# Attention into a two-layer feed-forward on one core: eight weight halves converted during the attention and kept in memory, six low parts moved to VectorE, and one step fewer in each conversion

## The chip, the cores and the metric

One core of a Trainium2 chip runs the whole program. The metric is the device time of one execution in microseconds (us). The kernel before takes 1147.3 us (median of three runs, 1147.26 to 1149.0). Differences up to 0.2%, about 2.3 us, are about what a measurement of this kernel cannot tell from no change.

The engines are named as in the profile: PE is TensorE's matrix product and PEld its weight load, DVE is VectorE, ACT is ScalarE, POOL is GpSimd, SP is the sync engine, whose queue issues nearly all transfers.

## The reference

A causal attention by blocks of 64, over 8 batches, 8 heads, 576 positions and head size 64; its output, as 4608 tokens of 512, goes through a feed-forward with 2048 hidden units and a leaky activation.

```python
scores = np.matmul(q, k.transpose(0, 1, 3, 2)) / np.sqrt(64)
scores = np.where(block_i >= block_j, scores, -1e9)
attn = np.exp(scores - scores.max(-1, keepdims=True))
attn = attn / (attn.sum(-1, keepdims=True) + 1e-09)
x = np.matmul(attn, v).transpose(0, 2, 1, 3).reshape(4608, 512)
h = x @ w_in
g = np.maximum(h, 0.0) + alpha * np.minimum(h, 0.0)
out = g @ w_out
```

The two weights reach the kernel as 64-bit floats, seen as pairs of 32-bit words. The kernel turns them into 32-bit floats itself.

## The kernel before, in words

**Products in two parts.** The kernel writes most operands of a product as a high part (a rounded copy, made on ACT) and a low part (the rest, a subtraction on POOL or DVE) and adds three products: high by high, low by high, high by low. `split` (L436) makes the two parts of a weight or of x: ACT at L438, POOL or DVE at L439.

**The hidden units in blocks.** The 2048 hidden units are 16 blocks f of 128. A block has two halves of weights, one of w_in and one of w_out, each 128 by 512. Blocks 0 to 5 (`first_weights`, L444) are converted at the start and stay in SBUF during the attention. The 32 pairs of heads (p = 0 to 31, four per batch) run through `query_tile` and `values`. Whenever the tokens of a batch are complete, chunks of 256 tokens (`chunk_a`, L634) go through blocks 0 to 5 between the steps of the attention (products at L518, L555) and their partial sums go to memory (`part`). x itself goes to memory too (`xd`).

**The second stage.** When the attention is over, its buffers are given back (`end_attention`, L1014), and blocks 6 to 15 are converted (`later_weights`, L460) while the last chunks of the first stage run; the w_in halves of blocks 6 and 7 alone have a low enough number (SOON) to be converted ahead, right behind the first six blocks. Then nine chunks of 512 tokens go through these ten blocks, two blocks at a time: `pair1` (L585) makes seven products in place of eight (L596) from sums and differences of quarters of the weights (L455) and of x (`factors`, L562), adds them on DVE (L605, L609), `activate` (L526) makes g (ACT L529, DVE L531), its high part gh (ACT L535) and its low part gl (POOL L538), and `ffn2` (L542) multiplies by w_out (L555). `store_out` (L1048) adds the partial sums.

**One conversion** (`to_f32`, L402) takes a half of 512 KB through six steps: DVE takes out the exponent (L416), ACT moves it (L419), DVE puts the sign on (L421), DVE takes out the mantissa as an integer into a PSUM bank (L425), ACT turns that integer into a float (L428), DVE adds the low word (L430) and multiplies by the power of two (L433). It holds two PSUM banks (eb, fb) from its first step to its last.

**What sets the order.** All this is a list of operations with priorities (the lower, the sooner). `Plan.schedule` runs through it with a cost for each operation, and for each engine, whenever that is free, takes the ready operation of lowest priority number for which buffers are free; buffers of the kinds in IN_ORDER are given in the order of the program. The result is one fixed order for each engine and for SP's queue. PSUM has eight banks, shared out by quotas: six for the attention (att), one each for the hidden units (hp) and the sums (acc); after the attention hp and acc have two each and the conversions four (words).

## Time and profile before

| | before |
|---|---|
| median of three runs | 1147.3 us |
| the profiled execution's own time | 1147.15 us |
| its span from first to last instruction | 1145.4 us |
| PE busy | 1119.7 us (98%) |
| PEld busy | 999.0 us (87%) |
| DVE busy | 844.1 us (74%) |
| ACT busy | 730.1 us (64%) |
| POOL busy | 612.1 us (53%) |
| transfers, mean | 127 GB/s |

Read it so: PE is idle for 25.7 us of the span, and where those lie decides what a change elsewhere can give. The stretches that matter are the start (0 to 120 us), the attention with the first six blocks (to about 596 us), the turn to the second stage (about 600 to 715 us, where blocks 6 to 15 are converted), and the second stage to the end.

### The profile page before, as it was taken

The numbers are of one execution on the slowest core, as the hardware profiler recorded it, in microseconds if no ns is written. First come the engines' busy times: TensorE is split into PE (matmuls) and PEld (weight loads), VectorE is DVE, ScalarE is ACT, GpSimd is POOL, SyncE is SP. The second block draws the span as 40 slices with busy tenths as digits, with TensorE's granted clock in tenths as the row PEclk, the third lists the DMA queues.
The fourth block names the chain that finished last, engine by engine and source line by source line (L and its number), as shares of the span: only waits on it lengthen the run. The fifth ranks groups of instructions, "written<-read, shape, count | busy, mean of one in ns | idle before, by whom it ended". The sixth has DMA issues, their size and how long they took to land. (4 is left out here: it accounts for less than half of the span.)

```text
span 1145.4 us, 22040 instructions
## 1 busy us (share of the span) xinstructions
PE 1119.7 (98%) x7288; PEld 999.0 (87%) x7288; DVE 844.1 (74%) x1968; ACT 730.1 (64%) x1950; POOL 612.1 (53%) x769
## 2 busy tenths in 40 slices
PE   7998999999999999999999989999999999999998
PEld 5666999999989999999998878988898889989887
DVE  8888899887887777778868999655657474656554
ACT  6887898987777887788865766443434343343432
POOL 5756556555565455556448987342425343342522
PEclk9999999999999999999999999999999999999999
DMA  8797676764745566557314442312122030302020
GB/s 229 218 258 234 172 215 175 205 176 113 228 133 151 163 180 183 132 142 226 88 48 165 144 143 74 116 37 74 41 71 78 34 111 1 111 16 95 2 74 37
DMA packets 74018, 145.86 MB, mean 127 GB/s; under 512 B 9648, under 2 KB 11440, under 8 KB 73904
## 3 DMA queue, kind: packets, MB, share of 16 engines
q1 hardware_dynamic: 73616, 144.31, 43.0%
q8 instruction: 58, 0.95, 0.4%
q14 instruction: 56, 0.46, 0.1%
q10 hardware_dynamic: 288, 0.14, 0.0%
HBM read 67.35 MB, written 28.31 MB: 84 GB/s over the span
## 5 line engine op out<-in xcount | busy, mean ns | idle before, releaser
L538 POOL TENSOR_TENSOR gl<-g,gh 128x256 fp32r<-128x256 f32 x288 | 223.2, 783 | 336.3 <-PE bank L596 159.6
L596 PEld LDWEIGHTS bank<-X,w 128*128 128x128 f32 x1890 | 253.6, 189 | 21.7 <-POOL X L439 1.1
L596 PE MATMUL bank<-X,w 128*128 128x256 f32 x1890 | 259.5, 281 | 1.3 <-POOL X L439 0.6
L555 PE MATMUL bank<-w,gh 128*128 128x512 f32 x720 | 225.8, 395 | 2.3 <-DVE g L531 1.3
L529 ACT ACTIVATE g<-bank 128x256 f32<-128x256 f32 x288 | 110.6, 385 | 158.2 <-DVE bank L609 142.0
L819 POOL TENSOR_SCALAR p<-p,ri 128x256 f32<-128x256 f32 (+3 forms) x256 | 146.0, 584 | 98.7 <-DVE ri L817 48.8
L535 ACT CAST gh<-g 128x256 fp32r<-128x256 f32 x288 | 116.9, 407 | 82.8 <-DVE g L531 81.6
L531 DVE SCALAR_TENSOR_TENSOR g<-g,oal,bank 128x256 f32<-128x256 f32 x288 | 136.0, 476 | 35.3 <-ACT g L529 29.4
L609 DVE TENSOR_TENSOR bank<-bank,g 128x256 f32<-128x256 f32 x180 | 76.0, 428 | 103.4 <-PE bank L596 102.4
L811 ACT ACTIVATE p<-bank,nm 128x256 f32<-128x256 f32 (+3 forms) x256 | 134.7, 531 | 27.0 <-DVE nm L808 11.8
L555 PE MATMUL bank<-w,gl 128*128 128x512 f32 x360 | 141.8, 394 | 1.4 <-POOL gl L538 1.4
L555 PE MATMUL bank<-wa,gh 128*128 128x512 f32 x432 | 140.9, 407 | 1.0 <-POOL wa L439 1.0
L555 PEld LDWEIGHTS bank<-w,gh 128*128 128x128 f32 x720 | 120.4, 188 | 15.4 <-DVE g L531 1.5
L518 PE MATMUL bank<-xh,wa 128*128 128x256 f32 x864 | 130.3, 288 | 0.0
L908 DVE TENSOR_TENSOR PL<-bank,PH 128x512 fp32r<-128x512 f32 (+2 forms) x189 | 111.1, 608 | 20.9 <-ACT PH L907 18.2
L518 PEld LDWEIGHTS bank<-xh,wa 128*128 128x128 f32 x864 | 114.1, 190 | 3.2 <-issue 0.4
L828 PE MATMUL bank<-ident,p 128*128 128x128 f32 x640 | 103.9, 280 | 6.6 <-POOL p L819 5.7
L795 PE MATMUL bank<-K,Q 128*128 128x512 f32 (+1 forms) x472 | 103.9, 335 | 0.0
L907 ACT CAST PH<-bank 128x512 fp32r<-128x512 f32 (+2 forms) x189 | 95.9, 529 | 11.8 <-PE bank L828 6.9
L828 PEld LDWEIGHTS bank<-ident,p 128*128 128x128 f32 x640 | 74.4, 142 | 19.7 <-POOL p L819 10.8
L605 DVE TENSOR_TENSOR g<-bank,g 128x256 f32<-128x256 f32 x135 | 56.6, 422 | 47.4 <-PE bank L596 46.5
L941 PE MATMUL bank<-PH,V 128*128 128x320 f32 x324 | 88.4, 288 | 0.0
(126 smaller groups left out, 2094.1 us busy)
## 6 DMA issues: line engine op xcount, KB each, us to landing
Q<-QH SPq DMA_DIRECT2D x62, 256.0 KB, 3.8
K<-KH SPq DMA_DIRECT2D x124, 128.0 KB, 3.6
vraw<-in_v SPq DMA_DIRECT2D x32, 320.0 KB, 3.1
qraw<-in_q SPq DMA_DIRECT2D x31, 320.0 KB, 3.6
xd<-xT SPq DMA_DIRECT2D x8, 1152.0 KB, 5.9
part<-o SPq DMA_DIRECT2D x36, 256.0 KB, 2.3
xb<-xd SPq DMA_DIRECT2D x9, 1024.0 KB, 5.3
m<-part SPq DMA_DIRECT2D x36, 256.0 KB, 3.3
```

The source lines that it names most:

```text
L518: nc.tensor.matmul(hp()[:, :n], ww()[:, 0, cc * P:(cc + 1) * P], x()[:, cc, :n], start=(i == 0 and cc == 0), stop=(i == 2 and cc == NCC - 1))
L529: op("ACT", c_act(CHA), lambda: nc.scalar.activation(out=g(), in_=hp()[:, ts], func=AF.Relu, scale=-1.0), r=[hp], w=[g], prio=FP)
L531: op("DVE", c_dve(CHA) + 60, lambda: nc.vector.scalar_tensor_tensor(out=g(), in0=g(), scalar=oal[:, f:f + 1], in1=hp()[:, ts], op0=ALU.mul ...
L535: op("ACT", c_act(CHA, True), lambda: nc.scalar.copy(out=gh(), in_=g()), r=[g], w=[gh], prio=FP)
L538: op("POOL", c_pool(CHA), lambda: nc.gpsimd.tensor_tensor(out=gl(), in0=g(), in1=gh().bitcast(F32), op=ALU.subtract), r=[g, gh], w=[gl], p ...
L555: nc.tensor.matmul(acc(), a()[:, ts], ww(), start=(first and i == 0), stop=(last and i == 2))
L596: nc.tensor.matmul(bank()[:, :CHA], W()[:, i, 256 * at + P * c:256 * at + P * c + P], B()[:, j, CHA * c:CHA * c + CHA], start=(n == 0), st ...
L795: nc.tensor.matmul(o, Q()[:, i, qs], K()[:, 2 * h + i, :w], start=(i == 0), stop=(i == 1))
L811: op("ACT", 238 + w / 1.2, lambda h=h, t=t: nc.scalar.activation(out=t()[:, :w], in_=sb[h]()[:, off[h]:off[h] + w], func=AF.Exp, bias=nm() ...
L819: op("POOL", 244 + w / 1.2, lambda h=h: nc.gpsimd.tensor_scalar(out=pts[h]()[:, :w], in0=pts[h]()[:, :w], scalar1=ri()[:, h:h + 1], scalar ...
L828: nc.tensor.transpose(out=tp()[:, base + c * P:base + (c + 1) * P], in_=pts[h]()[:, c * P:(c + 1) * P], identity=ident)
L908: op("DVE", c_dve(n) + (HALF if n == P else 0), lambda: nc.vector.tensor_tensor(out=lo(), in0=src(), in1=hi().bitcast(F32), op=ALU.subtrac ...
```

## The change

It has five parts.

1. In every conversion (32 halves) ACT's step L428 goes. DVE's next step reads the integer mantissa from PSUM and adds the low word times 2^-32; the last step, then a `scalar_tensor_tensor`, multiplies by 2^-20 and by the power of two.
2. Eight halves, those of w_in and w_out of blocks 8 to 11, are converted beside the attention, one each after pairs 12, 14, ... 26, with a priority number behind that of all nearby attention. Each result goes to a new tensor in memory (`wd`, 256 KB each), and `later_weights` loads it from there.
3. The low parts of the w_out halves of blocks 6 to 11 are subtracted on DVE and no longer on POOL.
4. After the attention hp has three banks and no longer two.
5. The plan is made anew with all this, so the order of every engine's work moves.

```diff
-BANKS, HB, AB, HT, AM, AT, WB = 6, 1, 1, 2, 2, 4, 4
+BANKS, HB, AB, HT, AM, AT, WB = 6, 1, 1, 3, 2, 4, 4
+AHEAD = {(8 + k // 2, k % 2): 12 + 2 * k for k in range(8)}
+    wd = dram.tile([2 * (NF - FA), P, 512], F32, name="wd")
...
-        op("ACT", c_act(512), lambda: nc.scalar.activation(out=fb(), in_=fb().bitcast(I32), func=AF.Copy, scale=2.0 ** -20),
-           w=[fb], prio=prio)
         op("DVE", c_dve(512), lambda: nc.vector.scalar_tensor_tensor(
-            out=mb(), in0=low(), scalar=2.0 ** -52, in1=fb(), op0=ALU.mult, op1=ALU.add),
+            out=mb(), in0=low(), scalar=2.0 ** -32, in1=fb().bitcast(I32), op0=ALU.mult, op1=ALU.add),
             r=[raw, fb], w=[mb], prio=prio)
-        op("DVE", c_dve(512), lambda: nc.vector.tensor_tensor(out=mb(), in0=mb(), in1=eb(), op=ALU.mult), r=[eb], w=[mb], prio=prio)
+        op("DVE", c_dve(512), lambda: nc.vector.scalar_tensor_tensor(
+            out=mb(), in0=mb(), scalar=2.0 ** -20, in1=eb(), op0=ALU.mult, op1=ALU.mult), r=[eb], w=[mb], prio=prio)
...
+    def weights_ahead(p):
+
+        for f, i in (k for k in AHEAD if AHEAD[k] == p):
+            pr = 5 * p + 100
+            mb, _ = to_f32((w_in, w_out)[i][f].bitcast(I32), pr, [("x", p // NP % 2, p % NP, 0, 1)])
+            at = 2 * (f - FA) + i
+            op("SP", 256, lambda mb=mb, at=at: nc.sync.dma_start(out=wd[at], in_=mb()), r=[mb], w=[("wd", f, i)], prio=pr)
+
+    def later(f, i, prio, after=(), use="att"):
+        if (f, i) not in AHEAD:
+            return to_f32((w_in, w_out)[i][f].bitcast(I32), prio, after, use)
+        mb, at = Buf("m"), 2 * (f - FA) + i
+        op("SP", 256, lambda: nc.sync.dma_start(out=mb(), in_=wd[at]), r=[("wd", f, i), *after], w=[mb], prio=prio)
+        return mb, mb
...
-                split(w, hi, lo, 512, [mb], (("w", f + i, 1), "h"), (("w", f + i, 1), "l"), [W], "POOL", prio(f) + .5)
+                split(w, hi, lo, 512, [mb], (("w", f + i, 1), "h"), (("w", f + i, 1), "l"), [W], "DVE" if f < 12 else "POOL", prio(f) + .5)
...
+        weights_ahead(p)
```

**The order, first place: DVE from the first sum of products in the second stage on.** `m` is a converted half, `raw` its words, `g` the hidden units, `X` a quarter of x. Before, in a row:

```order
L609 TENSOR_TENSOR bank_187<-bank_187,g_478 128x256
L439 TENSOR_TENSOR X_7981<-xt_7494,X_7981 128x512
L605 TENSOR_TENSOR g_687<-bank_221,g_478 128x256
L531 SCALAR_TENSOR_TENSOR g_610<-g_610,oal,bank_187 128x256
L416 TENSOR_SCALAR m_327<-raw_256 128x512
L425 TENSOR_SCALAR bank_247<-raw_256 128x512
L605 TENSOR_TENSOR g_7407<-bank_202,g_687 128x256
L605 TENSOR_TENSOR g_7429<-bank_240,g_687 128x256
L421 SCALAR_TENSOR_TENSOR bank_180<-raw_256,bank_180 128x512
L609 TENSOR_TENSOR bank_240<-bank_240,g_7407 128x256
L609 TENSOR_TENSOR bank_141<-bank_141,g_7429 128x256
L430 SCALAR_TENSOR_TENSOR m_327<-raw_256,bank_247 128x512
```

Now, from the same sum on (L609 is L625 there, L605 is L621, L531 is L547, L439 is L440):

```order
L625 TENSOR_TENSOR bank_188<-bank_188,g_7539 128x256
L621 TENSOR_TENSOR g_564<-bank_248,g_7539 128x256
L440 TENSOR_TENSOR X_8007<-xt_7567,X_8007 128x512
L547 SCALAR_TENSOR_TENSOR g_724<-g_724,oal,bank_188 128x256
L621 TENSOR_TENSOR g_505<-bank_142,g_564 128x256
L621 TENSOR_TENSOR g_7475<-bank_232,g_564 128x256
L625 TENSOR_TENSOR bank_232<-bank_232,g_505 128x256
L625 TENSOR_TENSOR bank_241<-bank_241,g_7475 128x256
L547 SCALAR_TENSOR_TENSOR g_7493<-g_7493,oal,bank_232 128x256
L625 TENSOR_TENSOR bank_203<-bank_203,g_505 128x256
L547 SCALAR_TENSOR_TENSOR g_7515<-g_7515,oal,bank_241 128x256
L547 SCALAR_TENSOR_TENSOR g_8083<-g_8083,oal,bank_203 128x256
```

Of the 24 rows from the first sum on, nine were steps of conversions; now two are. From the last row of the attention (L962) to the last step of the last conversion there were 173 rows of DVE with 18 conversions; now there are 137 with 10.

**Second place: DVE in the attention**, at the first of the eight halves. Before, the w_in halves of blocks 6 and 7 follow the first six blocks directly, and then no row of a conversion stands until the attention is over. Now these two come behind the eight, near the end of the attention, since `raw` and `m` are given in the order of the program. The first one's five DVE steps are spread over 24 rows, of which these are the last nine (L924 and L978 write parts of the attention's probabilities and outputs, L824 is a row maximum):

```order
L978 TENSOR_TENSOR xT<-bank_203,tmp_1312 64x320
L891 TENSOR_REDUCE sp_253<-s_138 128x1
L547 SCALAR_TENSOR_TENSOR g_564<-g_564,oal,bank_241 128x256
L893 RECIPROCAL ri_255<-sp_253 128x1
L430 SCALAR_TENSOR_TENSOR m_228<-raw_167,bank_248 128x512
L924 TENSOR_TENSOR PL<-bank_181,PH 128x2x128
L824 TENSOR_REDUCE nm_263<-bank_142 128x1
L824 TENSOR_REDUCE nm_263<-bank_188 128x1
L433 SCALAR_TENSOR_TENSOR m_228<-m_228,bank_232 128x512
```

The conversion takes the gaps that the attention leaves, and holds its two banks meanwhile; the longest of the eight spans 35 rows.

**Third place: SP's queue in the attention**, where it issues the loads of the next pair of heads. Before, in a row:

```order
L687 DMA K_128<-KL_323 64x512 x2
L672 DMA qraw_234<-in_q 128x640
L673 DMA kraw_245<-in_k 128x576
L659 DMA part<-o_164 128x512
L674 DMA vraw_170<-in_v 128x640
```

Now, at the second of the eight halves:

```order
L688 DMA qraw_235<-in_q 128x640
L689 DMA kraw_246<-in_k 128x576
L416 DMA raw_167<-in_w_in 128x1024
L675 DMA part<-o_154 128x512
L690 DMA vraw_171<-in_v 128x640
L703 DMA Q_126<-QH_293 64x2x512 x2
L703 DMA Q_126<-QL_320 64x512 x2
L688 DMA qraw_235<-in_q 128x640
L703 DMA K_128<-KH_315 64x512 x4
L703 DMA K_128<-KL_326 64x512 x2
L689 DMA kraw_246<-in_k 128x576
L467 DMA wd<-m_228 128x512
```

The queue runs in order: the store to `wd` waits for DVE's last step, and the next row behind it is a load of v.

## Rows read from the trace of the kernel before


**Rows 1.** busy time by stage: PE, PEld, DVE, ACT, POOL, TensorE clock, transfers

```profile
40.00:120.00 80.00, 75.58 (x427) 55.92 (x427) 68.71 (x160) 65.74 (x169) 48.70 (x55) 0.98 0.81 229
120.00:240.00 120.00, 119.25 (x857) 111.67 (x856) 107.22 (x286) 108.86 (x315) 74.00 (x105) 1.00 0.73 199
240.00:580.00 340.00, 337.48 (x2366) 313.26 (x2365) 273.26 (x690) 273.08 (x780) 192.04 (x261) 1.00 0.56 156
580.00:655.00 75.00, 73.29 (x479) 65.69 (x478) 59.28 (x106) 47.39 (x115) 57.09 (x64) 1.00 0.38 125
655.00:690.00 35.00, 29.95 (x177) 24.68 (x176) 33.50 (x62) 22.65 (x51) 30.38 (x30) 1.00 0.42 136
690.00:720.00 30.00, 30.00 (x192) 26.86 (x191) 25.83 (x53) 20.04 (x45) 25.00 (x26) 1.00 0.34 98
720.00:1140.00 420.00, 420.00 (x2623) 377.34 (x2622) 241.54 (x520) 163.17 (x406) 161.25 (x188) 1.00 0.17 57
1140.00:1145.40 5.40, 1.57 (x7) 0.94 (x5) 1.38 (x2) 0.00 (x0) 0.00 (x0) 1.00 0.38 146
```

**Rows 2.** timeline of PE, 655 to 690 us, rows with idle time before them

```profile
662.53 0.73 PE L596 MATMUL bank<-X,w 128*128 128x256 f32 x4 [0.16 <-ACT X L438]
663.89 2.21 PE L596 MATMUL bank<-X,w 128*128 128x256 f32 x14 [0.63 <-POOL X L439]
667.71 0.50 PE L555 MATMUL bank<-w,gl 128*128 128x512 f32 x1 [1.15 <-POOL gl L538]
672.79 0.73 PE L555 MATMUL bank<-w,gh 128*128 128x512 f32 x2 [1.04 <-ACT gh L535]
673.82 0.50 PE L555 MATMUL bank<-w,gl 128*128 128x512 f32 x1 [0.30 <-POOL gl L538]
681.21 0.73 PE L555 MATMUL bank<-w,gh 128*128 128x512 f32 x2 [1.27 <-DVE g L531]
688.34 0.97 PE L596 MATMUL bank<-X,w 128*128 128x256 f32 x6 [0.47 <-DVE g L531]
```

**Rows 3.** groups by line, 580 to 720 us: busy, mean ns, idle before

```profile
L439 POOL TENSOR_TENSOR w<-m,w 128x512 fp32r<-128x512 f32 x20 | 26.8, 1341 | 8.6 <-ACT w L438 8.6
L416 DVE TENSOR_SCALAR m<-raw 128x512 int32<-128x512 int32 x18 | 12.6, 698 | 2.4 <-issue 2.4
L419 ACT ACTIVATE bank<-m,ebias 128x512 int32<-128x512 int32 x18 | 12.5, 692 | 9.4 <-DVE m L416 9.2
L421 DVE SCALAR_TENSOR_TENSOR bank<-raw,bank 128x512 int32<-128x512 int32 x18 | 12.4, 691 | 2.7 <-ACT bank L419 2.6
L425 DVE TENSOR_SCALAR bank<-raw 128x512 int32<-128x512 int32 x18 | 12.3, 684 | 0.0
L433 DVE TENSOR_TENSOR m<-m,bank 128x512 f32<-128x512 f32 x18 | 12.2, 680 | 0.2
L430 DVE SCALAR_TENSOR_TENSOR m<-raw,bank 128x512 f32<-128x512 uint32 x18 | 12.2, 679 | 0.5 <-ACT bank L428 0.5
L428 ACT ACTIVATE bank<-bank 128x512 f32<-128x512 int32 x18 | 10.2, 568 | 0.0
```

**Rows 4.** line L439, one form on DVE: ns min/median/max

```profile
L439 DVE TENSOR_TENSOR X<-xt,X x18: 872/1170/1815, 619.2 to 1078.0; 128x512 fp32r<-128x512 f32 x18
```

**Rows 5.** waits of PE, 240 to 580 us: total, times, longest

```profile
PE bank L828 <- POOL p L819: 2.4, 4, 1.3
```

**Rows 6.** waits of SP's queue, whole span: total, times, longest

```profile
SPq L674 <- DVE xT L962: 52.2, 14, 7.1
```

**Rows 7.** timeline of PE and busy time by stage, 88 to 92 us

```profile
88.57 0.79 PE L555 MATMUL bank<-wa,gh 128*128 128x512 f32 x1 [0.99 <-POOL wa L439]
...
89.00:91.50 2.50, 2.50 (x12) 2.17 (x12) 1.52 (x5) 1.18 (x4) 2.34 (x5) 0.50 1.00 339
```

**Rows 8.** line L433, 80 to 150 us: ns min/median/max, first, last start

```profile
L433 DVE TENSOR_TENSOR m<-m,bank x5: 678/687/689, 84.1 to 125.2; 128x512 f32<-128x512 f32 x5
```

**Rows 9.** transfers, whole span: size, median us from issue to landing

```profile
m<-part SPq DMA_DIRECT2D x36, 256.0 KB, 3.3
```

More of the change, by code (lines that the diff above doesn't have):

```diff
@@ L464, in later_weights @@
             W = w1s[f] = Buf("w1")
-            ms = [to_f32(w_in[f + i].bitcast(I32), *((prio(f), ["att"], "words") if f > FA else (SOON, [], "att"))) for i in range(2)]
+            ms = [later(f + i, 0, *((prio(f), ["att"], "words") if f > FA else (SOON, [], "att"))) for i in range(2)]
             (m0, w0), (m1, w1) = ms
@@ L484, in later_weights @@
                 W = w2s[f + i] = Buf("w2")
-                mb, w = to_f32(w_out[f + i].bitcast(I32), prio(f) + .5, ["att"], "words")
+                mb, w = later(f + i, 1, prio(f) + .5, ["att"], "words")
                 hi, lo = ((lambda x=x, W=W: W()[:, x, :]) for x in range(2))
-                split(w, hi, lo, 512, [mb], (("w", f + i, 1), "h"), (("w", f + i, 1), "l"), [W], "POOL", prio(f) + .5)
+                split(w, hi, lo, 512, [mb], (("w", f + i, 1), "h"), (("w", f + i, 1), "l"), [W], "DVE" if f < 12 else "POOL", prio(f) + .5)
     fseq = [0]
```

## The prediction

> **What bounds the kernel now.** I read the busy time by stage first. PE is the engine to follow: from 690 to 1140 us it is busy for all of 450 us [rows 1], so whatever reaches 690 us sooner ends the kernel sooner by as much, and no other engine matters there. Idle time of PE is what a change can win. It lies in few places [rows 1]: 4.42 us in 40 to 120 us (80 less 75.58), 0.75 in 120 to 240, 2.52 in 240 to 580, 1.71 in 580 to 655, 5.05 in 655 to 690, and 3.83 in the last 5.4 us, where the last results are added and stored. Before 40 us the loads and the first pairs set the pace.
>
> Next I read PE's timeline in the worst stretch, 655 to 690 us. There are seven gaps, 5.02 us together [rows 2]. The reader is to see what ends them: the first two (0.79 us) wait for a part of x, the other five (4.23 us) for one step or another of the chain from a hidden unit's sum to its parts, DVE's g, ACT's gh, POOL's gl. In this stretch DVE is busy for 33.50 of 35 us, so the chain queues on DVE. POOL, with 30.38, is not far behind [rows 1].
>
> Then the groups by line say what fills DVE: 18 conversions with five steps of DVE, 0.698 + 0.691 + 0.684 + 0.679 + 0.680 = 3.43 us each [rows 3], 61.8 us of DVE's 118.6 between 580 and 720 us (59.28 + 33.50 + 25.83 [rows 1]). So the turn is bound by DVE, and by conversions above all. The order shows the same: of the 24 DVE rows from the first sum of products on, nine are steps of conversions.
>
> **The change part by part.** The sum is made against the profiled execution's own 1147.15 us (a span of 1145.4 and 1.75 around it); the median is 0.15 higher.
>
> *Eight conversions leave the turn.* DVE loses 8 x 3.43 = 27.5 us there, ACT 8 x (0.692 + 0.568) = 10.1 us [rows 3]. It gains the six low parts. The nearest row is DVE's other subtraction with both inputs in SBUF: 0.87 to 1.82 us, median 1.17 [rows 4], so 7.0 us, between 5.2 and 10.9. POOL loses 6 x 1.341 = 8.0 us [rows 3]. DVE is left with 20.5 us less of 118.6, and two conversion steps among the 24 rows. I take the five gaps of 4.23 us as gone and leave the two that wait for x (0.79), since x is still prepared as before. Of the 1.71 us in 580 to 655 I take half, 0.85: POOL, busy for 57.09 of 75 us there, is relieved by only a part of the six low parts that early. Together **-5.1 us**. The least is nothing, if another wait takes each place; the most is 5.05 + 1.71 = 6.8.
>
> *They enter the attention*, and two more with them: the w_in halves of blocks 6 and 7, which were converted by 126 us [rows 8], now come last of ten. So 240 to 580 us takes 34.3 us more on DVE, (273.26 + 34.3) / 340 = 90%, and 6.9 us more on ACT, 82%. The nearest row is 120 to 240 us: there DVE is at 89% and ACT at 91%, and PE idles 0.75 us in 120, which is 2.1 in 340, no more than the 2.52 it loses now [rows 1]. I take **0**. Below, the 2.52 could go. Above, each of the ten could cost a wait as long as the longest in this stretch, 1.3 us [rows 5], 13 us in all.
>
> *The start.* Twelve conversions lose ACT's 0.57 us, and 6.9 us of DVE move from about 100 us to later. One wait of PE there is for a weight, 0.99 us for a low part, and with the idle time before it goes a granted clock of 0.50, 1.2 GHz, from 89.0 to 91.5 us [rows 7], worth 1.25 us. The order is new here, so which wait goes cannot be said; I take the one that names a weight, **-1.0**. Below, all 4.42 us of idle time and the 1.25 could go (-5.7); above, the idle time could double (+4.4).
>
> *Edits at nothing.* ACT's step L428 in the turn: DVE waited 0.5 us for it in 18 conversions [rows 3]. The last step as scalar_tensor_tensor: L430 has that form already, 0.679 us against 0.680 [rows 3]. The reload of eight halves: a load of 256 KB lands in 3.3 us [rows 9]; it replaces one of 512 KB, and blocks 8 and 9 are wanted only when blocks 6 and 7 have been multiplied. If a buffer m comes free too late for that, the cover is gone and 3.3 us are lost once. A third bank for hidden units: it lets PE run one product ahead and is part of the gaps already counted.
>
> Sum: -5.1 + 0 - 1.0 = -6.1, so 1141.05 by the profiled execution, **1141.2 us** by the median.
>
> **The rivals.** What a measurement of this kernel can tell from no change is about 0.2%, 2.3 us: 1145.0 and 1149.6 are the bounds.
>
> *POOL is the next bound (0.17).* Of the gaps in the turn 1.45 us end with gl on POOL [rows 2], and POOL is busy for 30.38 of 35 us [rows 1]. Against it: POOL loses 8.0 us. If gl stays late, only the gaps that end with g and gh go (1.04 + 1.27 + 0.47 = 2.8 us), nothing before 655 us and nothing at the start: 1144.4, on the edge of what can be told. For it speaks how the moved subtraction behaves: DVE's takes 0.68 us with one input in PSUM [rows 3] and up to 1.82 with both in SBUF [rows 4], where POOL also reads. The Trainium skill (SBUF — State Buffer, Who interferes with whom) has a rule against this move: a VectorE instruction with two SBUF inputs and a GpSimd instruction that reads SBUF use one shared read port, and whichever starts second stands still until the first has finished. The spread in rows 4 agrees. By that rule alone the six would each hold up POOL's gl for their 0.68 us, 4.1 us in PE's gaps, and the sum would be -2.0, 1145.3.
>
> *Slower: the ten conversions stall the attention (0.11).* Each holds two of the attention's six banks from its first step to its last, which is now spread over 19 to 35 rows of DVE in the eight, and on SP's queue the store to memory stands ahead of a load of v, behind which wait the next pair's Q and K; that queue already waits up to 7.1 us at loads of v [rows 6]. So a late last step holds back a pair of heads. With 1.3 us each [rows 5] this costs 13 us: 1147.15 - 6.1 + 13 = 1154. It is slower by over 2.3 us from (6.1 + 2.3) / 10 = 0.84 us each on. Against it: PE has the first stage's products to fill with, and the waits of PE in 240 to 580 us are four [rows 5].
>
> *Nothing changes (0.06).* The converted halves are loaded into the same four buffers m, in the order of the program, behind block 6's and 7's w_out. If these set the pace, PE waits at the second pair of blocks for what it no longer waits for at the first: 1147.
>
> *The start gets better too (0.09).* All of the idle time of the turn (6.8 us) and of 40 to 120 us with the low clock (5.7) goes: 1134.7.
>
> **How the numbers follow.** My forecast has 0.57, its own range 1138 to 1144.8: the start's and the attention's bounds do not fall together. The range that should hold 8 times in 10 takes in the POOL rival, no change, and the nearer half of the better start: 1136 to 1147; it leaves out the slower rival (0.11) and the rest of the better start. Faster by over 0.2%: 0.57 + 0.09 + 0.10 of the POOL rival = 0.76. Within 0.2%: 0.07 + 0.06 = 0.13. Slower: 0.11.
>
> **What would show it.** In the changed profile PE's idle time between 655 and 690 us should be about 0.8 us, DVE's busy share from the end of the attention to 720 us lower by about a seventh, and the dense stretch of PE should begin about 6 us earlier. PE's idle time in 240 to 580 us should stay near 2.5 us; near 10 it shows the slower rival. If PE's gaps in the turn stay and name gl, POOL was the bound; if they stand at the second pair of blocks and name w, the buffers were. The low parts on DVE should take 0.9 to 1.8 us. The prediction is wrong if the turn does not shrink, or if what it gives is lost before 580 us.

## The result and the profile after

The changed kernel takes 1137.0 us (median of 4 runs, 1136.5 to 1139.1), the kernel before 1147.4 us beside it (4 runs, 1147.3 to 1149.0). The ratio is 0.991, with an interval of 0.9893 to 0.9927: 10.4 us or 0.9% faster. The forecast was 1141.2 us, 6.2 us faster, with a range of 1136 to 1147. The direction and the range held; the gain is larger than forecast by two thirds, and the profile tells where.

The profiled execution took 1136.95 us, with a span of 1135.2. First the page's busy time of each engine, after:

```profile
PE 1116.5 (98%) x7288; PEld 996.7 (88%) x7288; DVE 844.1 (74%) x1974; ACT 712.0 (63%) x1918; POOL 608.5 (54%) x763
```

PE's idle time falls from 25.7 to 18.7 us (1135.2 less 1116.5), and its busy time by 3.2 us. The two make up the 10.2 us of the span. ACT loses 18.1 us, 32 times the 0.57 us of its step [rows 3]. DVE's total is the same.

Now the busy time by stage, after. The columns are those of [rows 1]; the first six stages have the same bounds, and the dense stretch ends 10 us sooner:

```profile
40.00:120.00 80.00, 75.30 (x446) 56.25 (x447) 68.78 (x167) 63.64 (x170) 50.00 (x59) 1.00 0.86 236
120.00:240.00 120.00, 119.67 (x857) 112.30 (x856) 105.53 (x275) 104.99 (x301) 71.31 (x99) 1.00 0.69 191
240.00:580.00 340.00, 338.81 (x2376) 313.88 (x2376) 295.28 (x741) 279.63 (x792) 197.38 (x265) 1.00 0.62 175
580.00:655.00 75.00, 72.23 (x455) 63.12 (x455) 54.42 (x87) 39.34 (x95) 57.91 (x65) 1.00 0.43 135
655.00:690.00 35.00, 34.58 (x226) 31.13 (x225) 29.69 (x60) 21.39 (x50) 30.11 (x30) 1.00 0.24 80
690.00:720.00 30.00, 30.00 (x190) 26.89 (x189) 22.59 (x46) 14.80 (x36) 18.38 (x20) 1.00 0.39 126
720.00:1130.00 410.00, 410.00 (x2558) 368.26 (x2557) 232.40 (x500) 159.27 (x396) 157.03 (x183) 1.00 0.16 54
1130.00:1135.20 5.20, 1.38 (x6) 0.75 (x5) 1.38 (x2) 0.00 (x0) 0.00 (x0) 1.00 0.40 151
```

PE's idle time, before to after: 4.42 to 4.70 us in 40 to 120, 0.75 to 0.33 in 120 to 240, 2.52 to 1.19 in 240 to 580, 1.71 to 2.77 in 580 to 655, 5.05 to 0.42 in 655 to 690, and 3.83 to 3.82 at the end. The turn has lost the most, and 580 to 655 us has gained a wait.

A stage whose bounds are fixed in time is blurred when all the work shifts. So the text below uses two marks that are found in every kernel: the first and the last product of the probabilities' high part with V (the last field before the shapes). This is the line's row, of before and then of after:

```profile
L941 PE MATMUL bank<-PH,V x324: 220/308/415, 114.7 to 596.5; 128*128 128x320 f32 x108, 128*128 128x256 f32 x54
```

```profile
L957 PE MATMUL bank<-PH,V x324: 221/306/414, 109.9 to 591.2; 128*128 128x320 f32 x108, 128*128 128x256 f32 x54
```

**The start** (to the first V) goes from 114.7 to 109.9 us, 4.8 less. **The attention** (first to last V) goes from 481.8 to 481.3, 0.5 less. **The turn with all that follows** (last V to the end) goes from 1145.4 - 596.5 = 548.9 to 1135.2 - 591.2 = 544.0, 4.9 less. The forecast had -1.0, 0 and -5.1. By the marks two of its three terms came out in size, and the start is where it fell short.

But a new order can also move a product from one side of a mark to the other. So here is the busy time of the three parts, of before and then of after (columns as in [rows 1]):

```profile
0.00:114.70 114.70, 102.89 (x567) 73.56 (x568) 97.36 (x245) 91.16 (x235) 71.60 (x97) 0.99 0.82 235
114.70:596.50 481.80, 478.53 (x3376) 445.48 (x3375) 394.72 (x1012) 396.30 (x1131) 273.09 (x377) 1.00 0.58 161
596.50:1145.40 548.90, 538.31 (x3349) 479.95 (x3347) 351.97 (x714) 242.63 (x584) 267.38 (x295) 1.00 0.23 76
```

```profile
0.00:109.90 109.90, 99.78 (x563) 70.99 (x564) 94.53 (x244) 83.66 (x228) 70.53 (x97) 1.00 0.85 235
109.90:591.20 481.30, 479.77 (x3385) 446.34 (x3384) 414.89 (x1052) 400.07 (x1135) 279.43 (x379) 1.00 0.63 176
591.20:1135.20 544.00, 536.98 (x3345) 479.36 (x3343) 334.71 (x679) 228.28 (x557) 258.55 (x288) 1.00 0.22 73
```

Four products fewer stand ahead of the first V, nine more between the marks, and four fewer behind the last V. PE's idle time falls by 1.7 us in the start (11.81 to 10.12), by 1.7 in the attention (3.27 to 1.53) and by 3.6 behind it (10.59 to 7.02). Of the turn's 4.9 us, then, 1.3 are PE's busy time, about what the four products take. By idle time the turn gave less than its 5.1 us, and the attention gave more than nothing.

PE's timeline after, 575 to 720 us, rows with idle time before them, beside [rows 2]:

```profile
579.82 0.55 PE L844 MATMUL bank<-ident,p 128*128 128x128 f32 x3 [0.35 <-POOL p L835]
630.18 0.74 PE L571 MATMUL bank<-wa,gh 128*128 128x512 f32 x2 [1.58 <-ACT gh L551]
631.35 0.50 PE L571 MATMUL bank<-wa,gl 128*128 128x512 f32 x1 [0.43 <-POOL gl L554]
650.65 0.50 PE L571 MATMUL bank<-wa,gl 128*128 128x512 f32 x1 [0.60 <-POOL gl L554]
660.49 0.97 PE L612 MATMUL bank<-X,w 128*128 128x256 f32 x6 [0.15 <-POOL X L440]
661.73 0.50 PE L612 MATMUL bank<-X,w 128*128 128x256 f32 x2 [0.27 <-POOL X L440]
```

The five gaps of before that ended with g, gh or gl in 655 to 690 us are gone; the two that wait for x are left, with 0.42 us. PE runs without a gap from 662 us on; before it did so from 689 us on [rows 2], where the forecast had expected the dense stretch to begin about 6 us earlier. At 630 us, where the last products of the first six blocks (`wa`) stand, a wait of 1.58 us for gh is new.

The groups by line after, 580 to 720 us (columns as in [rows 3]):

```profile
L440 POOL TENSOR_TENSOR w<-m,w 128x512 fp32r<-128x512 f32 x14 | 18.8, 1342 | 1.6 <-ACT w L439 1.6
...
L418 DVE TENSOR_SCALAR m<-raw 128x512 int32<-128x512 int32 x10 | 7.7, 767 | 2.2 <-POOL gl L554 2.0
L440 DVE TENSOR_TENSOR w<-m,w 128x512 fp32r<-128x512 f32 x6 | 7.0, 1161 | 2.7 <-ACT w L439 2.6
L421 ACT ACTIVATE bank<-m,ebias 128x512 int32<-128x512 int32 x10 | 6.9, 690 | 6.0 <-DVE m L418 6.0
L427 DVE TENSOR_SCALAR bank<-raw 128x512 int32<-128x512 int32 x10 | 6.9, 689 | 5.6 <-DMA raw<-in_w_in 3.7 <-DMA raw<-in_w_out 1.9
L423 DVE SCALAR_TENSOR_TENSOR bank<-raw,bank 128x512 int32<-128x512 int32 x10 | 6.9, 689 | 1.7 <-ACT bank L421 1.5
L433 DVE SCALAR_TENSOR_TENSOR m<-m,bank 128x512 f32<-128x512 f32 x10 | 6.8, 679 | 0.1
L430 DVE SCALAR_TENSOR_TENSOR m<-raw,bank 128x512 f32<-128x512 uint32 x10 | 6.8, 678 | 0.0
```

Ten conversions stand in the turn instead of 18, each of six steps instead of seven (the list of steps in the kernel before names seven, five of them DVE's, though it says six). The step that now reads integers from PSUM (L430) takes 678 ns against 679, and the last step in its new form (L433) 679 against 680: both edits cost nothing. DVE waits no longer for ACT's step, but 5.6 us for raw words that are still on their way. The six low parts on DVE cost 7.0 us, as estimated.

Three more views of after. The spread of the six low parts (min/median/max in ns), the longest wait of PE in 240 to 580 us (total, times, longest), and the new transfers (size, median us from issue to landing):

```profile
L440 DVE TENSOR_TENSOR w<-m,w x6: 680/1016/1782, 615.4 to 635.1; 128x512 fp32r<-128x512 f32 x6
```

```profile
PE bank L844 <- POOL p L835: 0.6, 2, 0.4
```

```profile
wd<-m SPq DMA_DIRECT2D x8, 256.0 KB, 4.2
m<-wd SPq DMA_DIRECT2D x8, 256.0 KB, 3.3
```

The low parts take 0.68 to 1.78 us, where the forecast had 0.9 to 1.8. In the attention, where the ten conversions now stand, PE waits less than before [rows 5]. A half comes back from memory in 3.3 us, as did the load of the same size [rows 9].

### The profile page after: what moved, and what is told of

Its sections match the earlier page's. It is cut to its first block, busy times and chain, and to the rows that moved or that the text cites. A ratio compares the mean times of both kernels' runs of the same rounds, so it can differ in the third digit from the quotient of the medians.

```text
span 1135.2 us, 22037 instructions
## 1 busy us (share of the span) xinstructions
PE 1116.5 (98%) x7288; PEld 996.7 (88%) x7288; DVE 844.1 (74%) x1974; ACT 712.0 (63%) x1918; POOL 608.5 (54%) x763
## 4 chain that ended last, share of the span: by engine, by line
PE 87%; DVE 5%; POOL 3%; DMA 2%; ACT 1%; issue 1%; SPq 0%; POOLq 0%; ACTq 0%; DVEq 0%
PE bank L571 33%; PE bank L612 19%; PE bank L534 11%; PE bank L957 7%; PE bank L811 6%; PE bank L844 6%; PE bank L947 2%; PE bank L874 2%; PE bank L901 1%; DVE xh L520 1%; PE bank L806 1%; DMA Q<-QL 1%; POOL p L835 1%; POOL xl L522 0%; DVE PL L924 0%
## 5 line engine op out<-in xcount | busy, mean ns | idle before, releaser
L554 POOL TENSOR_TENSOR gl<-g,gh 128x256 fp32r<-128x256 f32 x288 | 220.7, 775 | 330.1 <-PE bank L612 164.7
L835 POOL TENSOR_SCALAR p<-p,ri 128x256 f32<-128x256 f32 (+3 forms) x256 | 150.6, 602 | 98.9 <-DVE ri L833 51.2
L547 DVE SCALAR_TENSOR_TENSOR g<-g,oal,bank 128x256 f32<-128x256 f32 x288 | 136.0, 476 | 36.9 <-ACT g L545 31.4
L625 DVE TENSOR_TENSOR bank<-bank,g 128x256 f32<-128x256 f32 x180 | 76.1, 428 | 104.9 <-PE bank L612 103.6
L827 ACT ACTIVATE p<-bank,nm 128x256 f32<-128x256 f32 (+3 forms) x256 | 134.8, 532 | 27.0 <-DVE nm L824 10.2
L924 DVE TENSOR_TENSOR PL<-bank,PH 128x512 fp32r<-128x512 f32 (+2 forms) x189 | 111.3, 608 | 13.2 <-ACT PH L923 10.9
L621 DVE TENSOR_TENSOR g<-bank,g 128x256 f32<-128x256 f32 x135 | 56.8, 422 | 47.9 <-PE bank L612 46.8
```

Source lines behind the costliest of these rows:

```text
L547: op("DVE", c_dve(CHA) + 60, lambda: nc.vector.scalar_tensor_tensor(out=g(), in0=g(), scalar=oal[:, f:f + 1], in1=hp()[:, ts], op0=ALU.mul ...
L554: op("POOL", c_pool(CHA), lambda: nc.gpsimd.tensor_tensor(out=gl(), in0=g(), in1=gh().bitcast(F32), op=ALU.subtract), r=[g, gh], w=[gl], p ...
L827: op("ACT", 238 + w / 1.2, lambda h=h, t=t: nc.scalar.activation(out=t()[:, :w], in_=sb[h]()[:, off[h]:off[h] + w], func=AF.Exp, bias=nm() ...
L835: op("POOL", 244 + w / 1.2, lambda h=h: nc.gpsimd.tensor_scalar(out=pts[h]()[:, :w], in0=pts[h]()[:, :w], scalar1=ri()[:, h:h + 1], scalar ...
L924: op("DVE", c_dve(n) + (HALF if n == P else 0), lambda: nc.vector.tensor_tensor(out=lo(), in0=src(), in1=hi().bitcast(F32), op=ALU.subtrac ...
```

## The experiments

Twelve kernels ran, in three groups of four; each group had its own runs of the kernel before, with medians of 1146.9, 1146.7 and 1147.2 us. Kernels of different groups are best compared by the table's last two columns. All of them compute the whole result.

Four theories stand in the expectations. **A** is the forecast's: each part gives in its own stretch, the eight halves in the turn and the removed step mainly at the start. **B**: what is gained, above all at the start, is mostly the luck of a new order, since every edit makes a new plan. **C**: the removed step of ACT gives the turn's gain, since it stood in the chain of every conversion. **D**, formed after eight runs: the turn gains only where the halves are ahead and hp has three banks, and the first pair of blocks starts near 660 us in kernels with ACT's step and near 655.5 without.

The table holds what the profiles show, of all but e1. "Step" is ACT's step, "ahead" the eight halves, "hp" the banks. Times are us. "Low" is what TensorE's low clock costs in the part to its left, taken from the busy time in stretches of 2.5 us: one less the granted clock, times the width.

| kernel | step | ahead | hp | to first V | low | first to last V | last V to end | low | median less before's | ratio, interval |
|---|---|---|---|---|---|---|---|---|---|---|
| before | kept | no | 2 | 114.7 | 1.7 | 481.8 | 548.9 | 0 | | |
| e7 (before, another order) | kept | no | 2 | 117.9 | 0 | 479.4 | 549.0 | 1.7 | +1.1 | 1.0012, 1.0002 to 1.0021 |
| e4 (before, two halves late) | kept | no | 2 | 114.1 | 1.7 | 482.7 | 552.0 | 1.7 | +2.3 | 1.0023, 1.0013 to 1.0034 |
| e9 | kept | yes | 2 | 116.6 | 3.4 | 482.4 | 548.9 | 1.7 | +0.6 | 1.0001, 0.9984 to 1.0017 |
| e11 | kept | no | 3 | 113.0 | 1.7 | 481.7 | 552.3 | 3.4 | +2.8 | 1.0026, 1.0009 to 1.0043 |
| e10 | kept | yes | 3 | 116.9 | 3.4 | 482.3 | 542.1 | 0 | -6.0 | 0.9945, 0.9925 to 0.9965 |
| e2 | kept | yes | 3 | 115.7 | 3.4 | 482.2 | 543.3 | 0 | -4.4 | 0.9958, 0.9944 to 0.9972 |
| e12 | gone | no | 2 | 113.3 | 1.7 | 483.3 | 550.3 | 3.4 | +0.8 | 1.0001, 0.9985 to 1.0016 |
| e3 | gone | no | 3 | 112.0 | 1.7 | 483.3 | 551.5 | 3.4 | +2.0 | 1.0016, 1.0007 to 1.0026 |
| e6 | gone | yes | 2 | 111.0 | 1.7 | 481.1 | 547.4 | 0 | -4.6 | 0.9959, 0.9944 to 0.9974 |
| after | gone | yes | 3 | 109.9 | 0 | 481.3 | 544.0 | 0 | -10.4 | 0.991, 0.9893 to 0.9927 |
| e5 (low parts on POOL) | gone | yes | 3 | 111.2 | 1.7 | 482.7 | 541.2 | 0 | -9.7 | 0.9915, 0.99 to 0.993 |
| e8 (after, another order) | gone | yes | 3 | 109.2 | 1.7 | 484.3 | 540.3 | 0 | -11.4 | 0.9901, 0.9887 to 0.9916 |

### The first group: one part alone, or all but one

**e1: the kernel before without ACT's step.**

```diff
-        op("ACT", c_act(512), lambda: nc.scalar.activation(out=fb(), in_=fb().bitcast(I32), func=AF.Copy, scale=2.0 ** -20),
-           w=[fb], prio=prio)
...
-            out=mb(), in0=low(), scalar=2.0 ** -52, in1=fb(), op0=ALU.mult, op1=ALU.add),
+            out=mb(), in0=low(), scalar=2.0 ** -32, in1=fb().bitcast(I32), op0=ALU.mult, op1=ALU.add),
...
-        op("DVE", c_dve(512), lambda: nc.vector.tensor_tensor(out=mb(), in0=mb(), in1=eb(), op=ALU.mult), r=[eb], w=[mb], prio=prio)
+        op("DVE", c_dve(512), lambda: nc.vector.scalar_tensor_tensor(
+            out=mb(), in0=mb(), scalar=2.0 ** -20, in1=eb(), op0=ALU.mult, op1=ALU.mult), r=[eb], w=[mb], prio=prio)
```

> The kernel before with ACT's step L428 left out of all 32 conversions and nothing else. Theory A (each part of the change gives in its own stretch; the step mainly helps the start): PE's idle time and low clock before 120 us fall by about 2 us, the turn (580 to 690 us, 6.8 us idle) stays above 5 us, in all 1144 to 1146 us. Theory B (the start's gain is only another order): the start moves by up to 3 us either way, 1144 to 1150. Theory C (the shorter conversion gives the turn, too): the turn's idle time falls below 4 us, 1141 or less.

Measured: 1148.1 us against 1146.9, ratio 1.0011 (1.0001 to 1.002). The execution that was profiled took 5399 us, several times as long as the others, so its trace says nothing, and the kernel ran again as e12. Alone, the removal gains nothing in the total. Theory A's 1144 to 1146 and theory C's 1141 or less both missed; theory B's 1144 to 1150 holds.

**e2: the change with ACT's step kept.** The same three places as in e1, the other way round:

```diff
+        op("ACT", c_act(512), lambda: nc.scalar.activation(out=fb(), in_=fb().bitcast(I32), func=AF.Copy, scale=2.0 ** -20),
+           w=[fb], prio=prio)
...
-            out=mb(), in0=low(), scalar=2.0 ** -32, in1=fb().bitcast(I32), op0=ALU.mult, op1=ALU.add),
+            out=mb(), in0=low(), scalar=2.0 ** -52, in1=fb(), op0=ALU.mult, op1=ALU.add),
...
-        op("DVE", c_dve(512), lambda: nc.vector.scalar_tensor_tensor(
-            out=mb(), in0=mb(), scalar=2.0 ** -20, in1=eb(), op0=ALU.mult, op1=ALU.mult), r=[eb], w=[mb], prio=prio)
+        op("DVE", c_dve(512), lambda: nc.vector.tensor_tensor(out=mb(), in0=mb(), in1=eb(), op=ALU.mult), r=[eb], w=[mb], prio=prio)
```

> The changed kernel with ACT's step put back in all conversions. Theory A: the turn stays as in the changed kernel (3 to 4 us idle), the start loses part of its gain: 1138 to 1140 us. Theory B: 1135 to 1141, with the difference before 120 us. Theory C: the turn's idle time comes back to over 5 us, 1141 or more.

Measured: 1142.5 us, ratio 0.9958 (0.9944 to 0.9972). The turn is as short as in after (543.3 against 544.0), so the step does not give the turn's gain. The start is as long as in the kernels before (115.7), but 3.4 us of it are low clock. The step's removal is worth 10.4 - 4.4 = 6.0 us on top of the rest, these 3.4 among them, though e1 gains nothing by it alone. Theory A's 1138 to 1140 missed. Theory C's total of 1141 or more came, but not its reason: from 580 to 690 us PE idles for 3.4 us, where C had over 5.

**e3: the change without the halves ahead.**

```diff
-AHEAD = {(8 + k // 2, k % 2): 12 + 2 * k for k in range(8)}
+AHEAD = {}
```

> The changed kernel with no half converted ahead: the shorter conversion, low parts on DVE and three hidden-unit banks alone; the w_in halves of blocks 6 and 7 are again converted by about 125 us. Theory A: most of the gain in the turn is gone, 655 to 690 us idle 3 us or more, 1142 to 1145 us. Theory C: the turn is as good as in the changed kernel, 1138 to 1140.

Measured: 1148.9 us, ratio 1.0016 (1.0007 to 1.0026). All of the gain is gone, more than theory A (1142 to 1145) or C (1138 to 1140) had expected. The turn takes 551.5 us, of which 3.4 are low clock.

**e4: the kernel before, with the w_in halves of blocks 6 and 7 converted only after pair 26**, where the change leaves them.

```diff
-            ms = [to_f32(w_in[f + i].bitcast(I32), *((prio(f), ["att"], "words") if f > FA else (SOON, [], "att"))) for i in range(2)]
+            ms = [to_f32(w_in[f + i].bitcast(I32), *((prio(f), ["att"], "words") if f > FA else (SOON, [("x", 0, 2, 0, 1)], "att"))) for i in range(2)]
```

> The kernel before, with the two w_in halves of blocks 6 and 7 converted only after pair 26 and no longer by 125 us; nothing else. Theory A (those two conversions delay the start): PE's idle time before 120 us falls by 1 to 2 us and the low clock at 89 us goes, 1144 to 1146 us. Rival: they were hidden, the start stays within 0.5 us, 1147 to 1148; if the turn suffers from their being late, more.

Measured: 1149.2 us, ratio 1.0023 (1.0013 to 1.0034). The start takes 114.1 us against 114.7. Taking the two halves out of the start, as the change does too, does not shorten it by itself: theory A's 1144 to 1146 missed. Its turn takes 552.0 us, of which 1.7 are low clock.

### The second group: the low parts, the bank, and the order

**e5: the change with the six low parts back on POOL.**

```diff
-                split(w, hi, lo, 512, [mb], (("w", f + i, 1), "h"), (("w", f + i, 1), "l"), [W], "DVE" if f < 12 else "POOL", prio(f) + .5)
+                split(w, hi, lo, 512, [mb], (("w", f + i, 1), "h"), (("w", f + i, 1), "l"), [W], "POOL", prio(f) + .5)
```

> The changed kernel with the six low parts of w_out back on POOL. If POOL is near its limit in the turn: PE's idle time with gl on POOL as releaser grows by 1 to 3 us between 600 and 700 us, 1138 to 1140 us. If the shared use of SBUF gives back what the move takes off POOL: 1136.5 to 1137.5.

Measured: 1137.0 us against after's 1137.0, ratio 0.9915 to before (0.99 to 0.993). That is the second of the two times expected; that the shared use of SBUF gives back what POOL gains is not shown by it. The move of the low parts is worth no more than another order is (e7 and e8 below). Its busy time in 655 to 690 us, columns as above:

```profile
655.00:690.00 35.00, 34.25 (x224) 30.79 (x223) 34.01 (x73) 22.86 (x52) 31.32 (x32) 1.00 0.38 121
```

POOL, with 31.32 of 35 us, was not the bound there. Nor does a busy DVE alone stop PE: with 34.01 us it is busier than in the kernel before (33.50 [rows 1]), and PE idles for 0.75 us.

**e6: the change with two banks for hp.**

```diff
-BANKS, HB, AB, HT, AM, AT, WB = 6, 1, 1, 3, 2, 4, 4
+BANKS, HB, AB, HT, AM, AT, WB = 6, 1, 1, 2, 2, 4, 4
```

> The changed kernel with two hidden-unit banks after the attention in place of three. If the third bank does nothing: 1136.5 to 1137.5 us. If it lets PE run ahead over the late gh and gl: the idle time in the turn grows from 3.2 to 4 to 6 us, 1138 to 1140.

Measured: 1142.1 us, ratio 0.9959 (0.9944 to 0.9974): taking the third bank away costs 5.1 us, or 5.8 with each measured against its own runs of the kernel before. The expectation had 1138 to 1140. PE's timeline of e6, 655 to 690 us, rows with idle time before them:

```profile
662.60 0.50 PE L571 MATMUL bank<-w,gl 128*128 128x512 f32 x1 [0.97 <-POOL gl L554]
667.17 0.74 PE L571 MATMUL bank<-w,gh 128*128 128x512 f32 x2 [0.47 <-ACT gh L551]
668.59 0.51 PE L571 MATMUL bank<-w,gl 128*128 128x512 f32 x1 [0.68 <-POOL gl L554]
675.47 0.98 PE L612 MATMUL bank<-X,w 128*128 128x256 f32 x6 [1.48 <-DVE g L547]
```

Here 3.60 us of gaps are back, and they name the same chain as [rows 2]: g, gh, gl. After has 0.42 us in this stretch, though its DVE is as busy (29.69 us there, 29.22 in e6). So what ended these gaps is not less work on DVE. The longest one stands ahead of a product of X by w that waited for DVE's g, the step that reads a hidden unit's bank; after has no such wait in this stretch. That is how a third bank should show: PE has another product to do while the chain runs.

**e7 and e8: another order alone.** A factor of the planner is moved a little, in the kernel before (e7) and in after (e8), and no instruction is added or taken away:

```diff
-LONGER = 1.12
+LONGER = 1.125
```

> The kernel before, computed alike, with a planner's factor on the costs of DVE, ACT and POOL of 1.125 in place of 1.12, so that the order is made anew and nothing else changes. Theory A: within 1.5 us of 1147.4, the low clock about 89 us may come or go. Theory B (an order's luck is worth as much as the start's gain): up to 4 us either way.

> The changed kernel, computed alike, with the same factor 1.125. Theory A: within 1.5 us of 1137.0. Theory B: up to 4 us either way, most of it before 120 us.

Measured: e7 1147.8 us, 1.1 above before, ratio 1.0012 (1.0002 to 1.0021); e8 1135.3 us, 1.7 below after, ratio to before 0.9901 (0.9887 to 0.9916). In these two tries a new order alone moves the time by 1 to 2 us. This speaks against theory B for the whole 10 us, but any difference of 1 to 2 us between two of these kernels may be no more than the order. Theory A had expected at most 1.5. e8 is the fastest of all kernels here.

### The third group: the halves ahead and the bank, apart and together

**e9: the kernel before with the halves ahead, and nothing else of the change.**

```diff
+AHEAD = {(8 + k // 2, k % 2): 12 + 2 * k for k in range(8)}
...
+    wd = dram.tile([2 * (NF - FA), P, 512], F32, name="wd")
...
+    def weights_ahead(p):
...
+    def later(f, i, prio, after=(), use="att"):
...
+        weights_ahead(p)
```

> The kernel before with the eight halves converted ahead and nothing else (ACT's step kept, low parts on POOL, two hidden-unit banks). Theory D (the time is the sum of two pieces: up to the first product of a pair of blocks, about 661 us with ACT's step and 655.5 without; from there to the end, 479.5 us with the halves ahead and three banks, 483.3 with the halves ahead and two, 485 to 491 without the halves ahead): 661 + 483.3 + 1.75 = 1146 us. Rival (the halves ahead carry the turn by themselves): 1142 to 1143.

Measured: 1147.8 us against 1147.2, ratio 1.0001 (0.9984 to 1.0017). Nothing is gained. Its busy time in 655 to 690 us, columns as above:

```profile
655.00:690.00 35.00, 30.02 (x164) 24.55 (x162) 31.46 (x54) 19.74 (x46) 27.17 (x27) 0.95 0.37 121
```

PE idles for 4.98 us, as much as in the kernel before (5.05 [rows 1]), although eight conversions have left DVE. Two of its gaps, again from PE's timeline:

```profile
666.04 1.36 PE L613 MATMUL bank<-X,w 128*128 128x256 f32 x8 [1.00 <-DVE X L441]
...
682.19 1.46 PE L613 MATMUL bank<-X,w 128*128 128x256 f32 x6 [2.44 <-DVE g L548]
```

The longest still ends with g, one step of the chain. So with two banks the chain is long enough to stop PE even where eight conversions are gone. That the conversions made it late in the kernel before, as the forecast has it, is not shown by any run. Theory D's 1146 us was too low: from the first product of a pair of blocks to the end it had 483.3 us, and 487.1 came, 1.7 of them low clock.

**e10: e9 with the third bank.**

```diff
-BANKS, HB, AB, HT, AM, AT, WB = 6, 1, 1, 2, 2, 4, 4
+BANKS, HB, AB, HT, AM, AT, WB = 6, 1, 1, 3, 2, 4, 4
```

> The kernel before with the eight halves converted ahead and three hidden-unit banks, nothing else. Theory D: 661 + 479.5 + 1.75 = 1142.3 us, and the place of the six low parts does not show. Rival (the low parts on DVE are needed where ACT's step is kept): 1144 or more.

Measured: 1141.2 us, ratio 0.9945 (0.9925 to 0.9965). The same stretch:

```profile
655.00:690.00 35.00, 32.72 (x201) 28.20 (x200) 32.69 (x64) 22.64 (x51) 29.64 (x30) 1.00 0.37 121
```

PE does 201 products there and not 164, and the turn takes 542.1 us against 548.9: 6.8 us less, of which 1.7 are a low clock that e9 has there. Theory D had 1142.3 us for the whole.

**e11: the kernel before with the third bank alone.**

```diff
-BANKS, HB, AB, HT, AM, AT, WB = 6, 1, 1, 2, 2, 4, 4
+BANKS, HB, AB, HT, AM, AT, WB = 6, 1, 1, 3, 2, 4, 4
```

> The kernel before with three hidden-unit banks after the attention and nothing else. Theory D: the third bank pays only where the weights come in time; without the halves ahead 1147 to 1152 us. Rival (the bank is worth its 4 us by itself): 1143.

Measured: 1149.9 us against 1147.2, ratio 1.0026 (1.0009 to 1.0043). The bank alone loses 2.8 us. Its busy time in two stretches, and then two rows of PE's timeline:

```profile
655.00:690.00 35.00, 33.14 (x214) 28.78 (x213) 34.39 (x69) 24.04 (x56) 28.57 (x31) 1.00 0.31 106
690.00:720.00 30.00, 24.98 (x130) 21.96 (x129) 22.60 (x40) 16.20 (x35) 21.94 (x22) 0.89 0.39 123
```

```profile
706.83 2.83 PE L596 MATMUL bank<-X,w 128*128 128x256 f32 x16 [2.18 <-POOL w L439]
714.99 5.17 PE L596 MATMUL bank<-X,w 128*128 128x256 f32 x29 [2.84 <-POOL w L439]
```

Up to 690 us PE is ahead of the kernel before, 33.14 us busy against 29.95. Then it has caught up with the weights: it waits 2.18 and 2.84 us for w, which is not converted yet, and the granted clock in this stretch is 0.89. So the bank moves the wait from the chain to the weights, and the halves ahead take that one away.

The conversions also came later than before. The last step of the twelfth, in the kernel before and then in e11:

```profile
669.64 0.67 DVE L433 TENSOR_TENSOR m<-m,bank 128x512 f32<-128x512 f32 x1
```

```profile
676.47 0.67 DVE L433 TENSOR_TENSOR m<-m,bank 128x512 f32<-128x512 f32 x1
```

The eleventh to the fourteenth are 3.0 to 6.8 us late. DVE did more work in between (69 instructions in 655 to 690 us, 62 before), and the quotas for hidden units, sums and conversions now add up to nine of PSUM's eight banks, so a conversion may also have had to wait for a bank. No run tells the two apart.

**e12: e1 again**, with the same diff:

```diff
-            out=mb(), in0=low(), scalar=2.0 ** -52, in1=fb(), op0=ALU.mult, op1=ALU.add),
+            out=mb(), in0=low(), scalar=2.0 ** -32, in1=fb().bitcast(I32), op0=ALU.mult, op1=ALU.add),
...
```

> The kernel before without ACT's step, the same as the first run, whose trace showed one far longer execution. Theory D: the first product of a pair of blocks starts about 655.5 us, some 5 us sooner than before, and all of it is lost from there to the end (about 490 us against 485), since the conversions end no sooner: 1147 to 1149. Rival: the start gains nothing by the step alone, 660 and 486.

Measured: 1148.0 us against 1147.2, ratio 1.0001 (0.9985 to 1.0016). Its start takes 113.3 us, 1.4 less than before's, and its turn 550.3 us, 1.4 more. Two low stretches of the clock stand in that turn, in its busy time by 2.5 us:

```profile
665.00:667.50 2.50, 1.87 (x12) 1.87 (x13) 2.50 (x5) 1.58 (x3) 2.50 (x3) 0.82 0.01 3
667.50:670.00 2.50, 2.50 (x9) 2.11 (x8) 2.50 (x6) 1.06 (x3) 1.80 (x3) 0.50 0.35 85
...
675.00:677.50 2.50, 2.42 (x13) 1.94 (x14) 2.50 (x6) 2.05 (x5) 2.50 (x3) 0.87 0.29 39
677.50:680.00 2.50, 2.50 (x10) 2.21 (x10) 2.50 (x5) 0.00 (x0) 2.50 (x3) 0.50 0.44 177
```

The first one loses 2.5 x (0.18 + 0.50) = 1.7 us, the second 2.5 x (0.13 + 0.50) = 1.6, with 0.1 more in the next stretch.

Theory D's statement that the turn gains only with the halves and the bank together holds in all four kernels, though its time for e9 was too low. Its other one, that the first pair of blocks starts near 660 us with ACT's step and near 655.5 without, fell: it started at 660.5 us in e12, which has no step, and at 657.2 in e11, which has it.

## Why the prediction was right, and where it was not

**The turn, -5.1: near in size, its reason half right.** It came to -4.9 us by the marks and to -3.6 by PE's idle time. The forecast said that the turn was bound by DVE and by conversions above all, and that without eight of them the five gaps that end with g, gh or gl would go. They went. But the halves alone leave 4.98 us of idle time (e9), and in e5 DVE is as busy as ever while PE idles for 0.75. So DVE's busy share was not what stopped PE, and the step that failed is in "edits at nothing": "A third bank for hidden units: it lets PE run one product ahead and is part of the gaps already counted." It is what the gaps depend on. Over two banks it is worth 5.1 us by the medians (e6 against after) and 6.6 in the kernel with ACT's step (e9 against e10); without the halves ahead it costs 1.2 us (e3 against e12, which differ in the place of the low parts too) to 2.8 (e11). In the table, last V to end takes 546.9 to 550.3 us less its low clock wherever one of the two is missing, and 540.3 to 544.0 in the five kernels with both. The forecast's number came out since the change has both: that part was luck.

**DVE in the turn.** Its busy time from 580 to 720 us fell from 118.6 to 106.7 us, a tenth and not a seventh (the forecast's own 20.5 of 118.6 us make a sixth). Its conversions take 10 x 3.5 = 35 us there instead of 61.8, and 7.0 us of low parts come in; since the work comes some 5 us earlier, more of the second stage now lies in this stretch. The first pair of blocks begins at 655.9 us, against 660.1.

**The half of 580 to 655 us did not come.** Taken as -0.85, it was +1.06 (1.71 to 2.77 us of idle time): the wait of 1.58 us for gh at 630 us is new. Between 655 and 690 us PE's idle time came to 0.42 us against 0.8 forecast. The idle time of both falls by 3.6 us, and the marks by 4.9. The rest of 1.3 us is in PE's busy time (538.31 to 536.98), with four products fewer behind the last V: they moved, and gave no gain of their own.

**The attention, 0: right to within 2 us.** DVE is busy for 295.28 of 340 us there, 87% against 90% forecast, and PE idles less than before: 1.53 us between the marks instead of 3.27, with nine more products there, which was not forecast. First to last V took 481.1 to 482.7 us in the six kernels with the halves ahead and the planner's usual factor, and 481.8 in before. The rival in which the ten conversions stall the attention had 1154 us; its waits did not come. On SP's queue the loads of v waited so (total, times, longest), beside [rows 6]:

```profile
SPq L690 <- DVE xT L978: 68.5, 15, 7.3
```

By this releaser the queue waited longer by 16 us. But that is one releaser among several: over all of them it waited for 83.7 us at the loads of v, 79.6 before, and at the eight stores to `wd` for 3.7 us in all. So the store that the rival feared held the queue up little, and PE not at all.

**The start, -1.0: mis-sized, -4.8 measured.** 1.7 us of it are the low clock: the kernel before has one such stretch, which [rows 7] shows in part, and after has none:

```profile
88.00:90.00 2.00, 2.00 (x18) 1.84 (x17) 1.24 (x3) 1.85 (x6) 0.91 (x1) 1.00 1.04 410
90.00:92.00 2.00, 2.00 (x9) 0.93 (x9) 1.91 (x10) 2.00 (x10) 0.62 (x2) 1.00 0.81 317
```

Of the other 3.1 us, 1.7 are idle time and 1.4 busy time, with four products fewer ahead of the first V. Less its low clock, the start takes 113.0 us in before, 111.3 to 113.5 in the other kernels with ACT's step (117.9 in e7, whose order differs), 110.3 and 111.6 without the step, and 107.5 to 109.9 without it and with the halves ahead. So without the halves the removed step gives 1.0 to 1.4 us there (e11 and e3, before and e12), and with them 2.4 to 4.0 (e2 and after, e9 and e6, e10 and e5). Each of these sizes is within the 4.9 us by which another order alone moved this mark (e7). The forecast saw the twelve steps of ACT and the 6.9 us of DVE that leave the start, yet took for them just one wait, as the only one that names a weight. That less work of ACT and DVE ahead of the first V brings all of it forward is the likely reason; no run shows it by itself. Why the step's removal seems to pay more with the halves ahead was not found.

**Edits at nothing.** L428 in the turn was right: with and without it the turn is as short (e2 against after). The reload and the new last step were right by their rows. The whole of the step's removal is not nothing: by the table's last but one column it is worth 3.7 to 6.0 us on top of the halves and the bank (e10 against e5, e2 against after), of which 1.7 and 3.4 are low clock at the start of the profiled executions. Alone it is worth nothing, since what e12 gains at the start it gives back in a turn with two stretches of low clock.

**POOL as the next bound (0.17): fell.** With the six low parts back on POOL the time is the same. The Trainium skill (SBUF — State Buffer, Who interferes with whom) says that a VectorE instruction with two SBUF inputs and a GpSimd instruction that reads SBUF use one read port and hold each other up. The trace agrees: of the six, two ran from 621.8 us on, while POOL stood idle to 623.1, and took 1.46 us together; the two of 1.78 us began at 615.4 and 635.1, while POOL was in a subtraction. In the kernel's time it was worth nothing, where the sum by that rule was 1145.3 us.

**Luck and the range.** The rival in which the start gets better too had 1134.7 us, and 1137.0 lies nearer to it than to the forecast. Of the 10.4 us, 1.7 are the one stretch of low clock, and 1 to 2 are within what another order does (e7, e8). The errors of the parts cancel in part: by idle time and low clock the start gave 3.4 us for 1.0, the attention 1.7 for nothing and the turn 3.6 for 5.1.

## What to carry to other kernels

A gap of the busiest engine that ends with a chain of other engines has two cures, a shorter chain and more work to do meanwhile, and each may be worthless without the other. When a change frees an engine and adds a buffer at once, price the buffer as a part of its own, and ask what the engine that runs ahead will meet next. Before a difference of 1 to 2 us is explained in a planned kernel, the same kernel should be run once in another order.

## What the runs showed of the hardware that was not expected

The granted clock falls to 0.50, the lower of its two levels (1.2 GHz), in separate stretches that cost 1.7 us each: two windows of 2.5 us with 0.71 and 0.60 in before, 0.82 and 0.50 in e12, and so in the others. In before, in e11 and in e12 PE had idled in the few us ahead: in before 1.23 and 0.99 us (the second in [rows 7]), in e11 2.18 and 2.84 us, each ahead of a stretch of its own, in e12 so 1.70 and 1.63 us. But a gap does not always bring it: after has one of 1.47 us at 70 us and one of 1.58 at 630, with a granted clock of 1.00. Such a stretch also differs between executions of one kernel: of after's four, three had a mean clock of 1.0 and took 1136.5 to 1137.0 us, one had 0.998 and took 1139.1. The forecast priced the one in the kernel before at 1.25 us, from a window that held only part of it.

An integer operand in PSUM cost DVE nothing more than a float one: 678 ns for 128x512 against 679.
